# Round-by-round batched stage in the first memory layer, and an earlier fetch in the two linear layers

## The chip, the cores and the metric

The kernel runs on one NeuronCore of a Trainium2 chip. The metric is the device time of one execution in microseconds (us). The kernel before took 3794.12 us, the median of three runs (3792.07 to 3799.89). One further execution was profiled: its span is 3778.8 us, and its own time was 3780.49 us. All durations below are from that execution.

## The reference

Four layers are applied to x, 2048 rows of 640 numbers in bf16, each with a residual: A, B, A, B.

```
x = x + A(layernorm(x));  x = x + B(layernorm(x))
x = x + A(layernorm(x));  x = x + B(layernorm(x))

A: for each of 64 segments of 32 rows:
     h = concat(mem, xs)             # 8 memory rows + 32 rows
     q, k, v = h @ Wq, h @ Wk, h @ Wv    # 32 heads of 192
     p = softmax(mask(q k^T * scale)); o = (p v) @ Wo
     mem = o[:8]; out = o[8:]        # the next segment needs mem
B: linear attention over all 2048 rows, 32 heads of 20
```

A is a recurrence: the 8 memory rows of a segment come out of the segment before. But q, k and v of the rows of x do not depend on the memory, and no earlier row of a segment looks at its last 8 rows. So the kernel computes q, k and v of these 8 rows for all 64 segments at once, ahead of the recurrence, and keeps the 8 memory rows and the first 24 rows (32 in all) for the recurrence itself.

## The kernel before

Layer A has two stages.

The batched stage (`A_pre`) computes q, k and v of the last 8 rows of all 64 segments, in two halves `h` of 32 segments (256 rows each). The weights are cut into four rounds `r` of 8 heads. One half of one round is called a unit below: there are 8. A unit multiplies K and Q (L787, twelve PSUM banks, each copied out once by `evict`), stores them to DRAM with one DMA of 1536 KB issued on ScalarE (L793, `kqb`), then multiplies V (L804, eight banks) and stores it with eight DMAs on GpSimd (L808, `vb`). So a unit has 20 copies out of PSUM, which alternate between VectorE (L87) and ScalarE (L89), and PSUM gives the stage eight banks. Before: half 0 goes through rounds 0, 1, 2, 3, then half 1 through 3, 2, 1, 0. Weights come on SyncE's queue. Three of five blocks of each matrix of rounds 0 and 3 share storage ("slots", loaded at L611; the others at L617), so each change between these two rounds loads nine blocks of 384 KB again.

In the first layer the stage also does the layernorm. The rows of half 0 are gathered first (`gather`, L691: four DMAs of 32 rows for each 128 rows), normalised (L221 to L244: VectorE statistics, two GpSimd casts, ScalarE Ln and Exp, VectorE scale), turned by TensorE (L166) and copied (`pt`). The rows of half 1, and all 16 blocks of 128 rows for the second stage, are normalised by small tasks: each `evict` runs the next task of a list, four tasks to a block (load, statistics, Ln and Exp, scale and store). The list is filled when half 0 reaches its third round. So tasks run with the copies 41 to 112 of 160.

The second stage (`A_chain`) is the recurrence over 64 segments, some 21 us each; its work on TensorE takes most of the span. It starts when the batched stage has ended.

In a layer B the beginning finishes layer A: the attention output of the last 8 rows of each segment has still to be multiplied by Wo. That is done in four parts `tb` of 16 segments (`post_steps`): `fetch` loads 1536 KB (L1117) and spreads it with four copies (recorded at L87 and L89, the lines of `Ev.copy`), `multiply` does 96 matmuls (L1129, L1130), copies the result (L1132, L1133) and stores it to `attn` (L1135). The fetched block and its spread form have two places each, used in turn. Beside it the first 512 rows are loaded, added to `attn` on GpSimd (L360), normalised (`norm_rows`) and, after the third multiply, turned by TensorE (`turn_rows`, L166, four blocks `ps_x` in a pool of three PSUM banks, copied by ScalarE). The instruction order of layer B is made by a scheduler; in the two stages of A it is kept as written, apart from DMA placement.

Of the kernel before, what the change touches and what calls it, by code (L numbers as in the profile page):

```python
# [8 lines left out]
P = 128  # L9
BF16 = mybir.dt.bfloat16  # L10
F32 = mybir.dt.float32
# [104 lines left out]
class Kernel:  # L116
# [131 lines left out]
    def layer_B(self, x_dram, at_dram, xout_dram, xnext_dram, li, bp, post):  # L248


        nc, tc, KC, D = self.nc, self.tc, self.KC, self.Dm
# [41 lines left out]
        with tc.tile_pool(name=f"B{li}_kv", bufs=1, space=bass.MemoryType.PSUM, reuse_waits="tile") as kvp, \  # L293
# [71 lines left out]
            def turn_rows(b, xn, xnT):  # L365
                pt = bank("ps_x", BF16)
                for k in range(KC):
                    self.transp(out=pt[:, P * k:P * k + P], in_=xn[:, P * k:P * k + P], identity=self.ident[:, :])
                q = P * (b % 4)
                self.ev.copy(out=xnT[:, :, q:q + P], in_=pt[:, 0:D].rearrange("p (k t) -> p k t", t=P), eng="s")  # L370

# [83 lines left out]
            with tc.issue_after(self.last_load.ins):  # L455
                load_rows(0)
            fetch, multiply = post
            ow = [fetch(tb) for tb in range(2)]
            for j in (1, 2, 0):
                nc.sync.dma_start(out=wqkv[:, :, D * j:D * j + D],  # L460
                                  in_=self.B_wqkv.rearrange("(k p) n -> p k n", p=P)[:, :, D * j:D * j + D])
            multiply(0, ow[0], kv_ps[0], side_bank("ps_post"))
            ow.append(fetch(2))
            rows = [norm_rows(b) for b in range(4)]
            multiply(1, ow[1], kv_ps[1], side_bank("ps_post"))
            ow.append(fetch(3))
            multiply(2, ow[2], kv_ps[0], side_bank("ps_post"))
            first_xnT = new_xnT()
            for b in range(4):
                turn_rows(b, rows[b], first_xnT)  # L470
            multiply(3, ow[3], kv_ps[1], side_bank("ps_post"))
            waiting = None
            for g in range(NG):
                xnT = first_xnT if g == 0 else norm_T(g)
                if g == 1:
                    late_constants()
                keys_values(g, xnT)
                if waiting is not None:
                    query_features(*waiting)
                waiting = (g, heads_T(xnT, 0, "qT"))  # L480
# [179 lines left out]
    def A_pre(self, xn_dram, li, load_matrix, piece, wo_mid, wo_end, lay_out_wo, early_wo, x_raw):  # L660
# [12 lines left out]
        with ExitStack() as es:  # L673
# [13 lines left out]

            def gather(dst, src, h, k):
                xv = src.rearrange("(s t) d -> t s d", t=32)
                for t2 in range(TP):  # L690
                    (nc.gpsimd if k % 2 else nc.scalar).dma_start(out=dst[SH * t2:SH * t2 + SH, :], in_=xv[24 + TP * k + t2, SH * h:SH * h + SH])  # L691

            def columns(h):
                return xT[h][:, 0:KC * T].rearrange("p (b t) -> p b t", t=T)
# [57 lines left out]
            if x_raw is not None:  # L752
                first = [norm_tasks(lambda x, k=k: gather(x, x_raw, 0, k),
                                    lambda xn, k=k: normed.__setitem__((0, k), xn)) for k in range(NT)]
                for step in zip(*first):
                    for f in step:
                        f()
            turn = nv = 0
            for h in range(NH):
                xBT = columns(h)  # L760
                for k in range(NT):
                    if x_raw is not None:
                        xb = normed[h, k]
                    else:
                        xb = xB[h][k % 2]
                        gather(xb, xn_dram, h, k)
                    transpose_rows(xb, h, k)

                if h == NH - 1:
                    lay_out_wo()  # L770
                for ri, r in enumerate(range(NR) if h == 0 and NH > 1 else range(NR - 1, -1, -1)):
                    st = sts[turn % 2]
                    turn += 1
                    if x_raw is not None and h == 0 and ri == 1:
                        self.build_A_consts()
                    if x_raw is not None and h + 1 < NH and ri == 2:
                        tasks += tails(h + 1)
                        tasks += all_rows()
                    for mi, m in enumerate("KQ"):
                        load_matrix(m, r)  # L780
                        w = [piece(m, r, b) for b in range(KC)]
                        for c0 in range(0, 12, CB):
                            ps = ps_.tile([P, 512], F32, name="ps_pre", tag="bank")
                            for i in range(CB):
                                c = c0 + i
                                for b in range(KC):
                                    nc.tensor.matmul(ps[:, T * i:T * i + T], lhsT=w[b][:, P * c:P * c + P], rhs=xBT[:, b, :],  # L787
                                                     start=(b == 0), stop=(b == KC - 1))
                            G, xi = c0 // 6, c0 % 6
                            so = st[:, :, 96 * mi:96 * mi + 96].rearrange("p s (i g t) -> p i g s t", g=2, t=8)  # L790
                            evict(out=so[:, xi:xi + CB, G],
                                  in_=ps[:, :].rearrange("p (i t s) -> p i s t", i=CB, t=8))
                    nc.scalar.dma_start(out=self.kqb_d[SH * h:SH * h + SH, :, r, :].rearrange("s p f -> p s f"), in_=st)  # L793
                    load_matrix("V", r)
                    if h == NH - 1 and ri == NR - 1:
                        early_wo()
                    w = [piece("V", r, b) for b in range(KC)]
                    for k in range(NT):
                        vt = vts[nv % 2]
                        nv += 1  # L800
                        for g in range(4):
                            ps = ps_.tile([P, 512], F32, name="ps_pre", tag="bank")
                            for b in range(KC):
                                nc.tensor.matmul(ps[:, 0:384], lhsT=xBT[:, b, P * k:P * k + P],  # L804
                                                 rhs=w[b][:, 384 * g:384 * g + 384], start=(b == 0), stop=(b == KC - 1))
                            evict(out=self.two_heads(vt[:, g, :]), in_=ps[:, 0:384].rearrange("p (e f) -> p e f", e=2))
                        for t2 in range(TP):
                            nc.gpsimd.dma_start(out=self.vb_d[SH * h:SH * h + SH, r, :, TP * k + t2, :],  # L808
                                                in_=vt[SH * t2:SH * t2 + SH, :, :].rearrange("p (g x) f -> p g (x f)", x=2))
            assert not tasks  # L810
# [297 lines left out]
    def post_steps(self, ops):  # L1108
# [5 lines left out]
        def fetch(tb):  # L1114
            o = 7680 + 12288 * (tb % 2)
            ot = low[:, o:o + 6144].rearrange("p (s f) -> p s f", f=384)
            nc.sync.dma_start(out=ot, in_=self.otb_d[16 * tb:16 * tb + 16].rearrange("s p f -> p s f"))  # L1117
            ow = low[:, o + 6144:o + 12288].rearrange("p (c q) -> p c q", q=P)
            for k in range(4):
# [16 lines left out]

        return fetch, multiply

# [34 lines left out]
```

## Time and profile before

| what | value |
|---|---|
| runs, median | 3794.12 us (3792.07 to 3799.89) |
| profiled span | 3778.8 us |
| TensorE busy in the span | 3556.3 us (94%) |
| batched stage of the first layer | 0 to 213.75 us |
| its first unit starts on TensorE | 14.29 us |
| TensorE idle between 14.29 and 213.75 us | 28.7 us |
| beginning of the first layer B (four multiplies) | 1604.84 to 1668.53 us |
| beginning of the second layer B | 3466.51 to 3531.28 us |

A line of the profile's order of time reads: start, duration, engine, source line, operation, what it writes and reads, how often, and in brackets how long the engine had been idle before and what ended that. "SPq", "ACTq" and "POOLq" are DMA issues of those engines. A line of the table of stretches reads: stretch, length, then for PE (matmul), PEld (weight load), DVE, ACT and POOL the busy time and in brackets the number of instructions, then the granted TensorE clock, the DMA share and GB/s.

### The profile page before, as it was taken

What the parts mean: (1) busy time and instruction counts of PE and PEld (TensorE: products, weight loads), DVE (VectorE), ACT (ScalarE), POOL (GpSimd) and SP (SyncE); (2) the same over time, 40 slices, a digit from 0 to 9 for tenths busy, and PEclk for the clock granted to TensorE, in tenths of its full rate; (3) what the DMA queues carried; (4) which work ended last, traced back from release to release, by engine and by line L of the source; (5) the groups of instructions that cost most, each with busy time, mean ns of one, the idle gap of its engine ahead of it and who ended that gap; (6) DMA issues with size and microseconds to landing.
All of it is one profiled execution on the core that took longest, in us unless ns stands there. A gap on an engine that the chain in (4) does not pass through costs nothing. (4 is left out here: it accounts for less than half of the span.)

```text
span 3778.8 us, 169108 instructions
## 1 busy us (share of the span) xinstructions
PE 3556.3 (94%) x71080; PEld 2322.3 (61%) x71408; DVE 2363.3 (63%) x6290; ACT 2072.3 (55%) x5285; POOL 1664.9 (44%) x4367
## 2 busy tenths in 40 slices
PE   7889999999999999989899899999999999999898
PEld 5666666666666666645468566666666666665453
DVE  3546666666666666645643566666666666664565
ACT  2246666656666666536432566666666666664553
POOL 2435555555554555430242454555555554553300
PEclk9999999999999999989899999999999999999899
DMA  9788787878878888840377888888788888889100
GB/s 327 238 261 290 275 297 270 291 276 279 296 273 287 279 289 285 299 143 1 121 245 199 292 284 283 293 280 289 274 294 276 290 286 275 294 276 312 53 1 29
DMA packets 532613, 935.26 MB, mean 248 GB/s; under 512 B 141178, under 2 KB 298378, under 8 KB 531850
## 3 DMA queue, kind: packets, MB, share of 16 engines
q1 hardware_dynamic: 393898, 805.73, 60.6%
q0 software_dynamic: 68288, 88.95, 8.0%
q10 hardware_dynamic: 69664, 29.76, 3.0%
q8 instruction: 558, 9.14, 1.0%
q14 instruction: 205, 1.68, 0.1%
HBM read 855.97 MB, written 72.09 MB: 246 GB/s over the span
## 5 line engine op out<-in xcount | busy, mean ns | idle before, releaser
L885 PE MATMUL ps_qk<-arena,hT 128*32 128x384 bf16 x20480 | 1002.9, 328 | 21.3 <-DMA arena<-in_A_Wk_dram 7.2
L885 PEld LDWEIGHTS <-hT 128*32 128x32 bf16 x30720 | 739.0, 96 | 439.7 <-DVE hT L1103 28.6
L895 ACT ACTIVATE raw<-ps_qk 128x384 bf16<-128x384 f32 x1024 | 502.0, 490 | 393.3 <-PE ps_s L993 250.9
L961 PE MATMUL ps_w<-arena,OT 128*32 128x160 bf16 x24576 | 545.1, 234 | 30.0 <-issue 16.3
L868 POOL DMA_DIRECT2D Vp<-vb x512 | 258.7, 505 | 655.6 <-PE ps_o L935 447.9
L885 PE MATMUL ps_v<-arena,hT 128*32 128x384 bf16 x10240 | 535.3, 329 | 0.0
L961 PEld LDWEIGHTS <-OT 128*32 128x32 bf16 x24576 | 434.5, 97 | 127.1 <-issue 49.0
L900 DVE STREAM_TRANSPOSE KT<-raw 128x384 bf16<-128x384 bf16 x512 | 296.2, 578 | 201.3 <-ACT raw L895 197.3
L903 DVE STREAM_TRANSPOSE QT<-raw 128x256 bf16<-128x256 bf16 x512 | 227.9, 445 | 239.0 <-ACT raw L895 196.8
L856 POOL DMA_DIRECT2D kqb<-kqb x512 | 290.0, 567 | 165.7 <-POOL KT L864 147.5
L916 DVE CAST Vp<-ps_v 64x384 bf16<-64x384 f32 x512 | 286.3, 559 | 89.0 <-ACT Vp L914 76.2
L954 POOL DMA_DIRECT2D otb<-otb x512 | 282.4, 552 | 123.0 <-DVE otb L950 102.2
L914 ACT ACTIVATE Vp<-ps_v 64x384 bf16<-64x384 f32 x512 | 246.1, 481 | 146.6 <-PE ps_v L885 109.3
L941 DVE CAST OT<-ps_o 128x192 bf16<-128x192 f32 x512 | 183.0, 358 | 217.8 <-PE ps_o L935 200.2
L1000 DVE TENSOR_TENSOR E<-E,ps_s 80x320 bf16<-80x320 bf16 x512 | 247.6, 484 | 73.4 <-ACT ps_s L999 69.3
L979 ACT ACTIVATE E<-ps_s 80x320 bf16<-80x320 f32 x512 | 221.5, 433 | 127.1 <-PE ps_s L927 99.0
L935 PEld LDWEIGHTS <-Vp 80*128 80x128 bf16 x4096 | 183.1, 99 | 156.3 <-issue 122.2
L935 PE MATMUL ps_o<-E,Vp 80*128 80x80 bf16 x4096 | 233.7, 202 | 22.9 <-ACT Vp L914 4.1
L927 PE MATMUL ps_s<-QT,KT 128*80 128x80 bf16 (+1 forms) x3072 | 234.3, 214 | 20.2 <-DVE KT L900 11.3
L849 ACT ACTIVATE Vp<-ps_w 32x160 bf16<-32x160 f32 x512 | 150.3, 294 | 177.8 <-DVE wt L1102 160.6
L940 ACT ACTIVATE OT<-ps_o 128x192 bf16<-128x192 f32 x512 | 167.7, 328 | 141.2 <-PE ps_o L935 141.2
L927 PEld LDWEIGHTS <-KT 128*80 128x80 bf16 x3072 | 196.2, 119 | 68.6 <-issue 58.9
(148 smaller groups left out, 5474.4 us busy)
## 6 DMA issues: line engine op xcount, KB each, us to landing
arena<-wo_rows SPq DMA_DIRECT2D x792, 320.0 KB, 6.8
arena<-in_A_Wq_dram SPq DMA_DIRECT2D x430, 384.0 KB, 4.7
arena<-in_A_Wv_dram SPq DMA_DIRECT2D x430, 384.0 KB, 6.4
arena<-in_A_Wk_dram SPq DMA_DIRECT2D x768, 192.0 KB, 4.7
kqb<-arena ACTq DMA_DIRECT2D x16, 1536.0 KB, 8.7
kqb<-kqb POOLq DMA_DIRECT2D x512, 48.0 KB, 5.1
arena<-in_A_Wk_dram SPq DMA_DIRECT2D x46, 384.0 KB, 7.1
vb<-arena POOLq DMA_DIRECT2D x128, 112.0 KB, 5.5
```

The source lines that it names most:

```text
L856: nc.gpsimd.dma_start(out=kqb[:], in_=self.kqb_d[s, :, r, :])
L868: nc.gpsimd.dma_start(out=Vs[n % 2][64:80, :], in_=self.vb_d[s, r].rearrange("g t f -> (g t) f"))
L885: nc.tensor.matmul(o[32 * g:32 * g + 32, 0:384], lhsT=hT[:, b, :], rhs=rhs, start=(i == 0), stop=(i == KC - 1), tile_position=(0, 32 * g), ...
L895: nc.scalar.activation(out=raw[:], in_=ps[:, 0:384], func=ACT.Copy)
L900: nc.vector.transpose(out=KT[:, :, 0:64], in_=raw[:, :].rearrange("p (c j) -> p c j", j=64))
L914: nc.scalar.activation(out=o, in_=i, func=ACT.Copy)
L916: nc.vector.tensor_copy(out=o, in_=i)
L927: nc.tensor.matmul(S[0:80, c0:c0 + 80 * (q1 - q0)], lhsT=KT[:, 3 * x + i, :], rhs=QT[:, x, q0:q1, :], start=False, stop=(x == 1 and i == 2 ...
L935: nc.tensor.matmul(O[x][:, 80 * i:80 * i + 80], lhsT=Vs[n % 2][0:80, 448 * x + k:448 * x + k + 128], rhs=E[0:80, 160 * x + 80 * e:160 * x ...
L954: nc.gpsimd.dma_start(out=self.otb_d[s, :, 96 * r:96 * r + 96], in_=otb[:, :, :].rearrange("p c t -> p (c t)"))
L961: nc.tensor.matmul(W[32 * g:32 * g + 32, 0:160], lhsT=OT[:, c, q:q + 32], rhs=w[:, 640 * i + 160 * g:640 * i + 160 * g + 160], start=(firs ...
L1000: nc.vector.tensor_tensor(out=E[0:80, 0:320], in0=E[0:80, 0:320], in1=rc, op=ALU.mult)
```

## The change

1. In the first layer the order of units becomes round 3 half 0, round 3 half 1, round 2 half 0, round 2 half 1, and so on to round 0. Layer three (the second A) keeps its order.
2. The eight gathers of half 0 are issued alternately on SyncE's and ScalarE's queues, ahead of the weights in SyncE's queue. Before, four went on ScalarE's and four on GpSimd's.
3. The list of tasks is filled at the first unit, so tasks run with the copies 1 to 72. The masks (`build_A_consts`) are built at the third unit instead of the second, and the two DMAs that lay out part of Wo (`lay_out_wo`) are issued at the fifth unit of the new order.
4. In both layers B `fetch` is split into `fetch` (the DMA) and `spread` (the copies). All four fetches are issued ahead of the loads of `wqkv`. The normalisation of the second 512 rows (`norm_T(1)`) is put after the last copy of the first 512 turned rows.

```diff
-                    (nc.gpsimd if k % 2 else nc.scalar).dma_start(out=dst[SH * t2:SH * t2 + SH, :], in_=xv[24 + TP * k + t2, SH * h:SH * h + SH])
+                    e = queues[t2 % 2] if queues else nc.gpsimd if k % 2 else nc.scalar
+                    e.dma_start(out=dst[SH * t2:SH * t2 + SH, :], in_=xv[24 + TP * k + t2, SH * h:SH * h + SH])
...
-                first = [norm_tasks(lambda x, k=k: gather(x, x_raw, 0, k),
+                first = [norm_tasks(lambda x, k=k: gather(x, x_raw, 0, k, (nc.sync, nc.scalar)),
...
+            if x_raw is not None:
+                steps = [(h, ri, NR - 1 - ri) for ri in range(NR) for h in range(NH)]
+            else:
+                steps = [(h, ri, ri if h == 0 and NH > 1 else NR - 1 - ri) for h in range(NH) for ri in range(NR)]
...
-                if h == NH - 1:
-                    lay_out_wo()
+                if (h, ri) == ((NH - 1, 0) if x_raw is None else (0, 2)):
+                    lay_out_wo()
...
-                    if x_raw is not None and h + 1 < NH and ri == 2:
-                        tasks += tails(h + 1)
-                        tasks += all_rows()
+                if x_raw is not None and (h, ri) == (0, 0):
+                    for h1 in range(1, NH):
+                        tasks += tails(h1)
+                    tasks += all_rows()
...
-            fetch, multiply = post
-            ow = [fetch(tb) for tb in range(2)]
+            fetch, spread, multiply = post
+            ot = [fetch(tb) for tb in range(2)]
+            ow = [spread(tb, ot[tb]) for tb in range(2)]
+            ot += [fetch(tb) for tb in range(2, 4)]
...
-            ow.append(fetch(2))
+            ow.append(spread(2, ot[2]))
...
-                turn_rows(b, rows[b], first_xnT)
+                turned = turn_rows(b, rows[b], first_xnT)
...
-                xnT = first_xnT if g == 0 else norm_T(g)
+                if g == 0:
+                    xnT = first_xnT
+                elif g == 1:
+                    with tc.issue_after(turned.ins):
+                        xnT = norm_T(g)
+                else:
+                    xnT = norm_T(g)
```

The built instruction lists have the same number of rows on TensorE, and on the other engines they differ only in the batched stage of the first layer and in the beginnings of the two layers B. SyncE's list loses nine slot loads and gains four gathers; GpSimd's loses four gathers.

## The prediction

> **What bounds the kernel now.** I read the page's busy shares first: TensorE is busy 94% of the span, so only 3778.8 - 3556.3 = 222 us can be won without taking work from it, and the change takes none. Then I looked for where TensorE idles in the parts that the change touches: the table of stretches, the order of time around each gap, and the waits of the batched stage.
>
> The table of stretches, one line for each unit of the first layer's batched stage in the order before (half 0 with rounds 0 to 3, half 1 with 3 to 0):
>
> ```profile
> 14.29:36.04 21.75, 21.75 (x160) 16.76 (x160) 6.40 (x11) 5.05 (x9) 2.13 (x4) 1.00 1.03 400
> 36.04:55.64 19.60, 19.60 (x162) 15.66 (x160) 6.39 (x10) 5.43 (x10) 5.64 (x24) 1.00 0.90 293
> 55.64:88.26 32.62, 22.72 (x162) 16.96 (x160) 8.98 (x22) 4.51 (x11) 7.27 (x18) 0.84 0.94 328
> 88.26:122.02 33.76, 22.33 (x170) 17.25 (x170) 20.56 (x56) 10.91 (x31) 17.78 (x43) 0.84 0.74 203
> 122.02:144.51 22.49, 22.49 (x161) 17.00 (x161) 12.84 (x33) 5.96 (x14) 7.02 (x19) 0.87 1.02 356
> 144.51:169.22 24.71, 20.66 (x162) 15.61 (x161) 13.23 (x37) 6.60 (x19) 10.15 (x25) 1.00 0.74 240
> 169.22:193.99 24.77, 21.44 (x161) 16.36 (x160) 9.68 (x19) 6.32 (x13) 13.09 (x27) 0.93 0.65 169
> 193.99:213.75 19.76, 19.76 (x166) 15.62 (x167) 6.38 (x10) 5.54 (x10) 4.22 (x8) 1.00 0.70 196
> ```
>
> A unit without disturbance takes 19.6 to 19.8 us. Units three to seven, which carry the normalisation tasks or their end, take up to 33.8. In the order of time one sees why:
>
> ```profile
> 8.52 0.89 DVE L221 BATCH_NORM_STATS2 ln_stats<-ln_x 128x6 f32<-128x320 bf16 x2 [5.67 <-DMA ln_x<-in_A_x_dram]
> ...
> 66.01 7.84 ACTq L691 DMA_DIRECT2D ln_x<-in_A_x_dram  x4
> 73.90 1.08 ACT L89 ACTIVATE arena<-ps_pre 128x512 bf16<-128x512 f32 x2 [17.57 <-DMA ln_x<-in_A_x_dram]
> 74.55 4.43 PE L787 MATMUL ps_pre<-arena 128*128 128x256 bf16 x20 [7.82 <-ACT arena L89]
> ...
> 122.02 16.15 PE L787 MATMUL ps_pre<-arena 128*128 128x256 bf16 x120 [9.12 <-ACT arena L89]
> ```
>
> The first statistics wait for the gathered rows until 8.52 us. Later ScalarE stands 17.6 us at the four gathers of half 1, behind weight traffic; PSUM fills and TensorE waits 7.8 us. At 122 us it waits 9.1 us for the turned rows of half 1. Two lines of the waits in this stage:
>
> ```profile
> DVE ln_stats L221 <- DMA ln_x<-in_A_x_dram: 42.2, 10, 16.4
> SPq L617 <- DMA kqb<-arena: 26.9, 2, 14.0
> ```
>
> VectorE, which also empties PSUM, waited 42.2 us in ten times for rows; and SyncE's weight loads waited 26.9 us for stores of `kqb` with which they share no data. In the built lists, the DMAs of SyncE and ScalarE share eight completion semaphores in rotation, so each waits for the one eight before it.
>
> In each layer B the turned rows of block 3 need a PSUM bank, whose copy on ScalarE stands behind the Ln of the next 512 rows:
>
> ```profile
> 1649.53 0.29 ACT L234 ACTIVATE ln_lv<-ln_mvr,eps 128x1 f32<-128x1 f32 x1 [6.63 <-POOL ln_mvr L227]
> ...
> 1653.08 2.48 ACT L89 ACTIVATE arena<-ps_x 128x640 bf16<-128x640 bf16 x4
> ...
> 1653.83 0.69 PE L166 MATMUL ps_x<-ident,arena 128*128 128x128 bf16 x5 [8.65 <-ACT arena L89]
> ...
> 3515.68 0.69 PE L166 MATMUL ps_x<-ident,arena 128*128 128x128 bf16 x5 [8.84 <-ACT arena L89]
> ```
>
> **What the Trainium skill says.** "DMA: Bandwidth & Descriptors", Anatomy of one DMA, gives a DMA a fixed cost of about 2 us beside its bytes, most of it the receipt of the write. The trace agrees for an unloaded machine (the fastest row load landed after 2.5 us); under the weight stream the median is 5.7 and the slowest 10.8, and those decide here. "TensorE: Matmul & The Clock Gate", What's actually happening: an idle window of about 3.4 us halves the clock until as long a busy one. The trace agrees: after the 8.65 us gap the L1129 matmuls take 0.63 us instead of 0.38 for 2.7 us. So a removed gap is worth more than its length.
>
> **The change part by part.**
>
> *The two layers B.* Removed: gaps of 8.65 and 8.84 us, and the cold matmuls after them. The 95 matmuls that follow take 14.2 and 15.1 us; at the pace of the 288 before them (39.3 us, 0.1365 each) they would take 13.0; so 1.2 and 2.1. Together 20.8 us. Added: SyncE's list now has fetches 1, 2, 3, then `wqkv`, then the first store to `attn`. Fetch 3 must wait for the spread of block 1, which ended at 1613.07 + 2.86 = 1615.9; behind it wait the three `wqkv` loads (6.8 us of issue), and behind them the `attn` store (at 1618.8 before), four row loads (1.85 us) and the `attn` rows. `wqkv` is first read at 1668, so its delay costs nothing. The rows landed at 1628.65; I put them at 1636 (1615.9 + 6.8 + store and landing 3 + issues 3 + load 7). Block 3 is added last, some 6 us later (four adds at 1.4), and is ready 3.5 us after that: about 1646, against transposes due at 1644. With its copy and the next transposes this leaves a gap of about 3 us in each; bounds 0.5 (rows in time, one copy) and 4.5. Net gain 2 x (10.4 - 3) = 15 us, from 12 to 20. The later normalisation is not needed before its transposes at 1706.7, 38 us on: nothing.
>
> *The start.* The gathers no longer share DMA with weights: eight issues of 0.44 us on two queues end near 2.7 us; with 2.5 us to land, statistics start near 5.2 for block 1 (8.52 and 9.62 before). The steps from there to the first matmul took 14.29 - 9.62 = 4.7 us, so it starts near 10.2 us. The five K blocks (2 MB at 400 GB/s is 5 us after about 3) are there by 10. Gain 4 us, bounds 2 and 5. It counts only through the tasks, next.
>
> *The stage.* Evictions are the measure: 160, at 0.99 us each when nothing disturbs (19.8/20). Before, the last task ran at 168.6; TensorE had then done 120 of 160, and 40 x 0.99 + about 5 for the set-up waits of the seventh unit gives 213.2 (traced 213.75). The same for after: tasks end with copy 72, TensorE is at most eight banks ahead, so 80 x 0.99 + 5 = 84 us remain. When do the tasks end? The two gathered blocks of half 1 come first; ScalarE's gathers are now ahead of any `kqb` store, so the 17.6 us stand goes; their statistics start near 17. Before, the first of the 16 blocks followed 10.5 us after that (76.16 to 86.66) and the 16 took 82 us (86.66 to 168.6). At that pace they end at 17 + 10.5 + 82 = 109.5. But the first eight now run beside the weight stream. Blocks whose load took 6.5 us there were 6.9 to 7.4 us apart instead of the mean 5.1, though the next one then followed after 3.5 to 3.9; I add 2 us, and 3 us for the masks (eighteen small GpSimd operations, 39.1 to 42.1 us before), now in the middle of the tasks. The turn to half 1 and its 9 us are inside the 82 and stay, now after unit one. Tasks end near 114, the stage at 198: 15 us earlier. Bounds: with the best eight blocks' pace (4.5 us) 100 and 184, a gain of 30; at 6.5 us a block 131 and 215, a loss of 2. In the 6.5 stands one thing more: in the built list the second `kqb` store on ScalarE waits for a V block of the third weight round, the 44th of 60. By the bytes moved in the trace before (18.7 MB by 55 us, 25.7 by 74.5) that lands between 60 and 67 us, against 45 to 56 for the store; copies wait behind it.
>
> *No cost or gain.* The nine slot loads (3.5 MB, 9 us of DMA) lay ahead of their use; no TensorE wait names a weight. The layout of Wo on ScalarE still lands (20.8 us) before the eighth unit. The recurrence's first `kqb` load now waits for the seventh unit's store: 9.0 + 5.5 us, inside the eighth unit's 19.8. The second A is unchanged.
>
> Sum: 15 + 15 = 30 us, 3778.8 to 3748.8 for the traced execution, which lay 13.6 us below the median of its timed sisters. On the median: 3794.1 - 30 = 3764.
>
> **The rivals.** *All of it (B):* tasks at 4.5 us, B full: 30 + 19 = 49, 3745. For: four blocks in uncrowded stretches took 17.3 and 18.5 us. Against: the first half of the tasks now lies in the most crowded stretch. *Only the layers B (C):* the tasks beside the weight stream eat the stage's gain: 3794 - 15 = 3779. For: the 42.2 us of waits for rows. *Slower (D):* one mechanism, VectorE standing at its row statistics while weights stream. It outweighs the 15 us of the layers B and 7.6 more only if the tasks end past 213.75 - 84 + 22.6 = 152 us, or (152 - 28)/16 = 7.8 us for every block; the worst four in a row took 23.8 us, 6.0 each. Then about 3805. *Not what it says (E):* the gaps in the layers B stay because block 3 comes later still, and the stage breaks even: 3792.
>
> **How the numbers follow.** A measurement of this kernel can tell 0.2%, 7.6 us, from no change. Forecast (A) 0.52, B 0.2, C 0.16, D 0.06, E 0.06. Faster: A, B and nearly all of C, 0.87; same: E and the rest, 0.07; slower 0.06. The range runs from B's time, 3745, to 3784, which holds C and its neighbours: gains of 10 to 49, the sum of the parts' bounds being 10 to 50.
>
> **What would show it.** First matmul of the stage near 10 us; no ScalarE stand of 17 us at gathers; the last row statistics near 111 us; the stage's end near 198; at ps_x gaps of 1 to 4 us in place of 8.7; the first spread of fetched block 2 after its landing near 1620. Wrong if the last statistics come past 130, if ps_x still waits 8 us, or if the recurrence, 21.7 us a segment, changes its pace.

## The result, and the profile after

The changed kernel takes 3771.39 us (median of four runs, 3766.23 to 3776.69) against 3793.1 us for the kernel before on the same chip: a ratio of 0.9942, with a 95% interval from 0.9918 to 0.9966. Timed once more beside later experiments it gave 0.9944 (0.9922 to 0.9966). So it is faster by 21 to 22 us, and the interval reaches from 13 to 31. The forecast was 30 us, a time of 3764.

The profiled execution spans 3764.5 us, 14.3 less than that of before. Where the stretches of the two traces differ:

| stretch, us | before | after | difference |
|---|---|---|---|
| start of the first unit on TensorE (inside the next line) | 14.29 | 10.19 | -4.1 |
| end of the batched stage, first layer | 213.75 | 198.01 | -15.7 |
| recurrence 1 | 1391.1 | 1396.3 | +5.2 |
| four multiplies, first layer B | 63.7 | 56.2 | -7.5 |
| rest of that layer B | 255.0 | 259.1 | +4.1 |
| batched stage of the second A | 160.0 | 160.0 | 0 |
| recurrence 2 | 1382.9 | 1386.6 | +3.7 |
| four multiplies, second layer B | 64.8 | 60.75 | -4.0 |
| rest of that layer B | 247.5 | 247.5 | 0 |

Not all of this is the change. Over fourteen traces of this study the two recurrences together took from 2767 to 2791 us, with no relation to which parts were in: stage_only below has 2780, a second trace of the changed kernel 2782, another variant 2767. Their 5.2 and 3.7 us are spread. The 15.7 us are not, as the experiments show. The rest of the first layer B lies anywhere from 255.6 to 264.3 us in seven traces with the changed layers B, so its 4.1 us alone would say little; but they hold a new gap, shown below.

The table of stretches of the changed kernel, its first six units (round 3 half 0, round 3 half 1, round 2 half 0, and so on):

```profile
10.19:40.48 30.29, 22.65 (x171) 17.42 (x171) 14.77 (x38) 8.18 (x21) 8.64 (x24) 0.92 1.05 380
40.48:62.62 22.14, 22.14 (x161) 16.81 (x161) 12.73 (x33) 5.08 (x12) 6.92 (x18) 0.88 0.95 338
62.62:91.87 29.25, 22.07 (x161) 16.46 (x160) 12.57 (x34) 6.50 (x18) 12.76 (x42) 0.94 0.98 358
91.87:115.53 23.66, 21.14 (x160) 15.56 (x160) 15.91 (x44) 7.97 (x23) 11.29 (x28) 1.00 0.72 206
115.53:139.12 23.59, 20.08 (x161) 15.62 (x160) 9.68 (x19) 6.15 (x13) 9.05 (x17) 1.00 1.04 315
139.12:158.72 19.60, 19.60 (x162) 15.64 (x160) 6.38 (x10) 5.54 (x10) 4.21 (x8) 1.00 0.68 201
```

The tasks now lie in the first four units, and from the sixth on a unit takes 19.6 us. The worst units were 32.6 and 33.8 us before and are 30.3 and 29.3 now. The clock column matters too: over the first 250 us its mean went from 0.911 to 0.945, and 0.034 x 250 / 3778.8 = 0.0022 is most of the rise of the mean clock between the kernels (from 0.9769 in 21 executions of the kernel before to 0.9795 in six of the changed one in the same session). It goes with the stage: in the two traces with the old stage it is 0.911 over these 250 us, in the twelve with the new one 0.925 to 0.952.

In the order of time, the same places as in the prediction:

```profile
3.48 0.89 DVE L221 BATCH_NORM_STATS2 ln_stats<-ln_x 128x6 f32<-128x320 bf16 x2 [0.64 <-DMA ln_x<-in_A_x_dram]
...
16.86 0.89 DVE L221 BATCH_NORM_STATS2 ln_stats<-ln_x 128x6 f32<-128x320 bf16 x2 [0.17 <-DMA ln_x<-in_A_x_dram]
...
40.48 15.80 PE L803 MATMUL ps_pre<-arena 128*128 128x256 bf16 x120 [7.64 <-ACT arena L89]
...
68.76 0.87 ACT L89 ACTIVATE arena<-ps_pre 128x384 bf16<-128x384 f32 x2 [9.42 <-DMA arena<-in_A_Wv_dram]
...
111.91 0.88 DVE L221 BATCH_NORM_STATS2 ln_stats<-ln_x 128x6 f32<-128x320 bf16 x2
```

Statistics start at 3.5 instead of 8.5 us, those of half 1 at 16.9, the last come at 111.9 instead of 165.6. The 17.6 us stand at the gathers is gone. In its place ScalarE stands 9.4 us before 68.76, and what ends it is a landed block of Wv: the second `kqb` store waits for a weight load with which it shares no data, as forecast. VectorE's waits for rows fell from 42.2 us to this, in the waits of the stage:

```profile
DVE ln_stats L221 <- DMA ln_x<-in_A_x_dram: 17.9, 12, 3.1
```

In the two layers B, at the turned rows of the third and the fourth block of 128 rows (blocks 2 and 3):

```profile
1635.43 0.45 PE L166 MATMUL ps_x<-ident,arena 128*128 128x128 bf16 x5 [1.52 <-ACT arena L246]
1637.37 0.44 PE L166 MATMUL ps_x<-ident,arena 128*128 128x128 bf16 x5 [1.26 <-ACT arena L89]
...
3499.10 0.45 PE L166 MATMUL ps_x<-ident,arena 128*128 128x128 bf16 x5 [3.27 <-ACT arena L246]
3501.04 0.69 PE L166 MATMUL ps_x<-ident,arena 128*128 128x128 bf16 x5 [1.26 <-ACT arena L89]
```

The gaps of 8.65 and 8.84 us became 1.52 + 1.26 = 2.8 and 3.27 + 1.26 = 4.5. But a new gap stands 30 us further on. Here are GpSimd, VectorE and TensorE of the first layer B:

```profile
1657.58 4.02 POOL L328 TENSOR_SCALAR_AFFINE_SELECT arena<-arena 128x720 bf16<-128x720 bf16 x4
1661.57 5.43 POOL L360 TENSOR_TENSOR arena<-arena 128x640 bf16<-128x640 bf16 x4
1662.99 0.89 DVE L221 BATCH_NORM_STATS2 ln_stats<-arena 128x6 f32<-128x320 bf16 x2 [5.06 <-POOL arena L360]
1664.76 1.47 DVE L409 TENSOR_REDUCE sk<-arena 128x64 f32<-128x1280 bf16 x1
1668.01 0.47 PE L428 MATMUL kv<-arena 128*120 128x126 bf16 x2 [5.27 <-DVE arena L422]
```

The first `kv` matmul waits 5.27 us for VectorE. VectorE's next product for it, the sums at L409, is queued behind statistics (L221) which wait for GpSimd's additions (L360) of the last 512 rows, and those are queued behind constants that GpSimd builds for layer B (L317 to L328, 8.3 us in all). Here are GpSimd's first constant and TensorE's first `kv` matmul in the kernel before, and the same constant after:

```profile
1667.07 1.38 POOL L317 MEMSET arena<- 128x1536 bf16 x1 [0.78 <-PE kv L1129]
1681.87 0.46 PE L428 MATMUL kv<-arena 128*120 128x126 bf16 x2 [1.06 <-DVE arena L422]
...
1653.22 1.38 POOL L317 MEMSET arena<- 128x1536 bf16 x1
```

Before, the matmul waited 1.06 us, and GpSimd itself waited for TensorE's multiplies: L317 starts 1.5 us before they end. After, it follows GpSimd's own casts without a gap, 2.8 us after the multiplies have ended. The multiplies end 7.5 us earlier than before, counted from their start, L317 starts only 3.3 us earlier. The difference of 4.2 us is the new gap and the +4.1 in the table.

### The profile page after: what moved, and what is told of

Same layout as the page of the kernel before. It is cut to its first block, busy times and chain, and to the rows that moved or that the text cites. A ratio compares the mean times of both kernels' runs of the same rounds, so it can differ in the third digit from the quotient of the medians.

```text
span 3764.5 us, 169123 instructions
## 1 busy us (share of the span) xinstructions
PE 3547.2 (94%) x71064; PEld 2322.7 (62%) x71408; DVE 2365.1 (63%) x6290; ACT 2072.6 (55%) x5285; POOL 1658.2 (44%) x4363
## 4 chain that ended last, share of the span: by engine, by line
PE 56%; DMA 12%; DVE 8%; issue 8%; ACT 6%; PEld 4%; POOL 4%; SPq 0%; POOLq 0%; DVEq 0%; ACTq 0%
PE ps_qk L901 18%; PE ps_w L977 8%; PE ps_v L901 7%; DMA arena<-wo_rows 5%; PE ps_o L951 4%; PE ps_s L943 4%; PEld L803 3%; DVE hT L857 3%; PE ps_s L1009 2%; DMA Vp<-vb 2%; PE ps_s L938 2%; PE ps_idle L984 2%; PE ps_qk L388 2%; PE ps_pre L803 1%; DVE E L1016 1%
## 5 line engine op out<-in xcount | busy, mean ns | idle before, releaser
L932 DVE CAST Vp<-ps_v 64x384 bf16<-64x384 f32 x512 | 286.1, 559 | 90.0 <-ACT Vp L930 76.3
L1016 DVE TENSOR_TENSOR E<-E,ps_s 80x320 bf16<-80x320 bf16 x512 | 247.5, 483 | 73.3 <-ACT ps_s L1015 69.3
L943 PEld LDWEIGHTS <-KT 128*80 128x80 bf16 x3072 | 196.1, 120 | 71.3 <-issue 59.4
```

Of the source, the lines that this page charges most:

```text
L932: nc.vector.tensor_copy(out=o, in_=i)
L943: nc.tensor.matmul(S[0:80, c0:c0 + 80 * (q1 - q0)], lhsT=KT[:, 3 * x + i, :], rhs=QT[:, x, q0:q1, :], start=False, stop=(x == 1 and i == 2 ...
L1016: nc.vector.tensor_tensor(out=E[0:80, 0:320], in0=E[0:80, 0:320], in1=rc, op=ALU.mult)
```

## The experiments

Each run is given as a ratio to the kernel before on its own chip, since one of the chips was faster for both. Differences in us are worked out from the ratios.

| run | ratio, 95% interval | us | stage end | idle B1 | idle B3 |
|---|---|---|---|---|---|
| changed kernel, first | 0.9942 (0.9918 to 0.9966) | -22 | 198.0 | 42.2 | 29.3 |
| stage_only | 0.9973 (0.9960 to 0.9985) | -10 | 200.9 | 43.5 | 33.0 |
| layersB_only | 0.9992 (0.9984 to 1.0001) | -3 | 212.9 | 40.3 | 28.6 |
| issue_only | 0.9974 (0.9960 to 0.9988) | -10 | 199.2 | 42.5 | 33.3 |
| fetch_only | 0.9966 (0.9955 to 0.9978) | -13 | 198.6 | 41.1 | 32.3 |
| old_gathers | 0.9968 (0.9958 to 0.9979) | -12 | 201.9 | 41.0 | 28.9 |
| late_store | 0.9956 (0.9942 to 0.9970) | -17 | 196.1 | 40.7 | 27.7 |
| masks_late | 0.9958 (0.9943 to 0.9972) | -16 | 198.6 | 41.1 | 31.0 |
| consts_early | 1.0018 (1.0010 to 1.0027) | +7 | 198.8 | 54.4 | 36.0 |
| after_again | 0.9944 (0.9922 to 0.9966) | -21 | 198.3 | 41.7 | 30.3 |
| consts_dve | 0.9927 (0.9906 to 0.9947) | -28 | 198.9 | 39.4 | 28.5 |
| combo_w | 0.9934 (0.9911 to 0.9958) | -25 | 196.1 | 40.0 | 28.6 |
| rows_late | 0.9957 (0.9945 to 0.9970) | -16 | 197.9 | 41.7 | 29.6 |

"Idle" is the sum of TensorE's gaps between matmul records from the first multiply of the layer B to the first matmul of the next batched stage, or to the end of the run (43.5 and 32.4 us before); it leaves out the clock, which moves the length of a layer B by several us from one execution to the next. The times of single executions of one kernel lie up to 26 us apart, so a traced stretch decides below where a few us are asked for.

**stage_only.** The changed stage with the old layers B.

```diff
-            ot = [fetch(tb) for tb in range(2)]
-            ow = [spread(tb, ot[tb]) for tb in range(2)]
-            ot += [fetch(tb) for tb in range(2, 4)]
+            ow = [spread(tb, fetch(tb)) for tb in range(2)]
...
-                elif g == 1:
-                    with tc.issue_after(turned.ins):
-                        xnT = norm_T(g)
```

> Only the changes in the first layer's batched stage (order of units, gathers, task list); both layers B as before. My theory, that the two parts are independent and add up: the stage ends at 198 us as in the changed kernel, the gaps of 8.7 us at ps_x in both layers B are back, and the time falls by 15 us (11 to 19) against the kernel before. Rival, that a busier TensorE in the stage is paid back in the recurrence (4 us more between the first segment and the first layer B in the changed kernel's trace): the recurrence is again 4 us longer than before and the gain is 11 us or less. Rival, that those 4 us are only spread between executions: the recurrence lies anywhere from -4 to +5 us of before's, with no relation to which parts are in.

Measured: 10 us faster (6 to 15), the stage ends at 200.9 (198.0 to 199.2 in six other traces with the same stage), the gaps at `ps_x` are back with 9.27 and 9.46 us. The recurrences took 1390.6 and 1389.4 us: nothing of a payback in the first. Its rest of the first layer B took 259.3 us with the same idle time as before (43.5); here it is the pace of the matmuls, not a wait, that differs.

**layersB_only.** The old stage with the changed layers B.

The edit is the layer B part of the change, as its diff shows it, on the kernel before.

> Only the changes in the two layers B; the batched stage as before. My theory: stage ends at 213.8 us, the four multiplies take 56 us in the first and 61 us in the second layer B (63.7 and 64.8 before), the time falls by 11.5 us as the traces of before and after show (15 as predicted). Rival of the payback: the first recurrence is as before (nothing in the stage changed) and the 4 us in the rest of the first layer B (the stretch after the multiplies, 255.0 before and 259.1 after) come with the later normalisation of rows 512 to 1023, so only 7 us are gained. Rival of the spread: the rest of the layer B is within 1 us of 255.

Measured: 3 us faster at best guess, between 6 faster and 0.4 slower. The multiplies took 59.5 and 57.6 us, so the gaps fell as in the changed kernel. But the new gap in front of `kv` is there, 3.06 and 3.44 us, and the rest of the first layer B took 258.1. The rival that the gain is partly given back behind the multiplies is right in its result; its reason, the later normalisation, is taken up further on. Together with stage_only this makes 13 us, 8 less than the changed kernel measured twice; their intervals overlap, and no run tells whether the two parts help each other or the executions drew apart.

**issue_only and fetch_only.** Half of the change of the layers B each: only the later normalisation (issue_only: the three lines of `fetch` and `spread` as in the diff of stage_only), or only the early fetches (fetch_only):

```diff
-                elif g == 1:
-                    with tc.issue_after(turned.ins):
-                        xnT = norm_T(g)
```

> The changed kernel, with fetches 2 and 3 back at their old places and only the normalisation of the second 512 rows put later. My theory: ScalarE's copy of the turned block no longer stands behind the Ln, which was the whole gap of 8.7 us; the rows of attn land earlier (1629 instead of 1636 on before's scale), so block 3 is there in time and the gap at ps_x is only 1.3 us, with none in front of the L246 result; but fetch 2 then starts behind wqkv as before, hidden. The time is 2 to 5 us below the changed kernel's, the multiplies take 55 to 57 us in both layers B. Rival, that the early fetches are what removes the gap: the gap is 5 us or more and the time is 5 to 8 us above the changed kernel's in each layer B.

> The changed kernel, with the fetches early but the normalisation of the second 512 rows not put later. My theory: the copy of ps_x stands behind the Ln again, the gap is 8 us or more in each layer B, and as the early fetches win nothing by themselves (they were hidden) and delay the rows of attn, the time is 12 to 20 us above the changed kernel's. Rival, that the early fetches carry the gain: the gap stays below 3 us and the time is that of the changed kernel, within 4 us.

Both missed their numbers. The first lines are TensorE of fetch_only:

```profile
1632.96 0.45 PE L166 MATMUL ps_x<-ident,arena 128*128 128x128 bf16 x5 [1.69 <-ACT arena L246]
1639.08 0.69 PE L166 MATMUL ps_x<-ident,arena 128*128 128x128 bf16 x5 [5.45 <-ACT arena L89]
```

The next are ScalarE and TensorE of issue_only:

```profile
1649.35 0.29 ACT L234 ACTIVATE ln_lv<-ln_mvr,eps 128x1 f32<-128x1 f32 x1 [6.25 <-POOL ln_mvr L227]
1651.97 1.56 ACT L89 ACTIVATE arena<-ps_qk 120x512 bf16<-120x512 f32 x3
1652.61 2.72 PE L388 MATMUL ps_qk<-arena 128*120 128x512 bf16 x6 [6.28 <-ACT arena L89]
```

Without the later normalisation 7.1 us of the 8.7 remain. With it alone the gap at `ps_x` is gone altogether, the multiplies take 53.5 us in both layers, and 6.3 us come back at `ps_qk`: ScalarE's copies of those banks now stand behind the Ln of the third 512 rows, which wait for their rows of `attn`. Idle time is then that of the kernel before (42.5 and 33.3 against 43.5 and 32.4). It is the same blocking, one group of rows later. Only both halves together leave less idle time in both layers. A count from a common start says the same: from the first multiply to the first `kv` it is 77.7 and 78.0 us in issue_only, 76.3 and 76.6 in fetch_only, 77.0 to 78.8 in two traces with the old layers B, and 73.3 to 75.2 in seven with both halves.

**old_gathers.** The gathers of half 0 where they were.

```diff
-                first = [norm_tasks(lambda x, k=k: gather(x, x_raw, 0, k, (nc.sync, nc.scalar)),
+                first = [norm_tasks(lambda x, k=k: gather(x, x_raw, 0, k),
```

> The changed kernel, with the eight gathers of half 0 back on ScalarE's and GpSimd's queues. My theory: the first matmul of the stage starts near 14 us instead of 10.2, the tasks start 4 us later and the last row statistics come near 116 us instead of 112, so the stage ends at 202 us instead of 198 and the time is 4 us above the changed kernel's. Rival, that the start is hidden: the tasks are bound by the loads of rows and the weight stream from 20 us on, the last row statistics stay at 112 us and the stage ends within 1 us of 198.

TensorE of its beginning:

```profile
14.35 15.29 PE L803 MATMUL ps_pre<-arena 128*128 128x256 bf16 x120 [0.79 <-ACT arena L89]
```

The stage ends at 201.9. The start moved by 2.9 to 4.2 us and the end by 3.6 to 3.9 against the changed kernel's two traces (starts at 10.19 and 11.44, ends at 198.0 and 198.3). Five more traces with the new gathers and the same stage end at 198.6 to 200.9, so the end alone would not decide. Counted from its first matmul the stage takes 187.6 us here and 186.9 to 189.7 in those seven traces: it is no shorter for the late start. The start is not hidden. The last row statistics came at 113.8 us and not near 116, so about half of the delay was made up there, and the end moved all the same.

**late_store.** The second unit's `kqb` store, issued behind the third unit's K copies.

```diff
-                nc.scalar.dma_start(out=self.kqb_d[SH * h:SH * h + SH, :, r, :].rearrange("s p f -> p s f"), in_=st)
+                    while held and mi == 0:
+                        held.pop()()
+                def store(h=h, r=r, st=st):
+                    nc.scalar.dma_start(out=self.kqb_d[SH * h:SH * h + SH, :, r, :].rearrange("s p f -> p s f"), in_=st)
+                if x_raw is not None and (h, ri) == (1, 0):
+                    held.append(store)
+                else:
+                    store()
```

> The changed kernel, with one DMA moved in ScalarE's list: the store of kqb of the second unit is issued behind the third unit's K copies, instead of ahead of the second unit's V copies, where ScalarE stood 9.4 us until 67.9 us. My theory, that the stand and the copies queued behind it delay the tasks: the stand is gone or below 2 us, the last row statistics come 7 us (4 to 9) earlier, at 105 us, and the stage ends 7 us (4 to 9) earlier, at 191. Rival, that the stand only takes the place of waits for the rows under the weight stream: the wait of VectorE for ln_x, 17.9 us in the changed kernel, grows by as much, and the stage ends within 2 us of 198. Rival, that the store meets its lane again: the stand comes back later, with the same end.

The stand of 9.4 us is gone, and the stage ends at 196.1: 2 us earlier than in the changed kernel's first trace and 3 earlier than the mean of the seven traces with its stage (199.0), not 7. The rival is mostly right. The waits of the stage show where the rest went:

```profile
DVE ln_stats L221 <- DMA ln_x<-in_A_x_dram: 22.1, 13, 4.4
ACT arena L89 <- DVE ln_stats L221: 3.3, 1, 3.3
ACT arena L89 <- DMA arena<-in_A_Wq_dram: 2.6, 1, 2.6
```

VectorE's wait for rows grew by 4.2 us, and two short stands of ScalarE at `kqb` stores, 3.3 and 2.6 us, came in (the view puts them down to other instructions, but each ends with the issue of a `kqb` store, at 88.33 and 80.32 us). A stand of 9.4 us was worth 2 to 3.

**masks_late.** The masks built behind the tasks.

```diff
-                if x_raw is not None and h == 0 and ri == 1:
+                if x_raw is not None and h == 0 and ri == 2:
                     self.build_A_consts()
```

> The changed kernel, with the masks (build_A_consts, 3.3 us of GpSimd at 77 us, between the casts of the tasks) built at the fifth unit, behind the tasks. My theory, with the 3 us of the prediction: the last row statistics come 3 us earlier, at 109, and the stage ends at 195. Rival, that GpSimd has slack there (it waits 2 us or more for VectorE's statistics in most blocks): the last row statistics stay within 1 us of 112 and the stage's end within 1 us of 198.

The last statistics came 0.9 us earlier (111.0), the stage ended at 198.6 against 198.0 and 198.3; both lie within the spread of the traces. The rival is right: GpSimd has slack there, and the 3 us of the prediction are nothing.

**rows_late.** The tasks of the 16 blocks listed later.

```diff
                     for h1 in range(1, NH):
                         tasks += tails(h1)
+                if x_raw is not None and (h, ri) == (0, 1):
                     tasks += all_rows()
```

> The changed kernel, with the tasks for the 16 blocks listed at the second unit (the eight tasks of half 1 stay in the first), so that they lie with copies 21 to 84 instead of 9 to 72 and fewer of them beside the weight stream. Theory A, that each block has its price wherever it lies: the last row statistics come 12 copies later, at 121 to 124 us, with 68 copies x 0.99 + 5 us left the stage ends at 195 to 198, within 3 us of the changed kernel's. Theory B, that the weight stream makes the tasks dearer (the 2 us of the prediction and the stand at the store): the stage ends 4 us or more earlier, at 194 or less. Theory C, that TensorE idles in the first unit for want of tasks, no matter where they are: it ends later, at 201 or more.

The text misnames the place: (0, 1) is the third unit, so these tasks lie with the copies 41 to 104, and its 121 to 124 us don't apply. The last statistics came at 147.0. Still the stage ends at 197.9, within 0.4 us of the changed kernel, which is theory A's result. Its reason, one price for a block wherever it lies, is not shown: two gaps changed places. Here are TensorE and VectorE:

```profile
33.71 13.26 PE L804 MATMUL ps_pre<-arena 128*128 128x256 bf16 x120 [0.79 <-ACT arena L89]
...
72.33 0.89 DVE L221 BATCH_NORM_STATS2 ln_stats<-ln_x 128x6 f32<-128x320 bf16 x2 [14.86 <-DMA ln_x<-in_A_x_dram]
74.07 9.01 PE L821 MATMUL ps_pre<-arena 128*128 128x384 bf16 x40 [7.50 <-DVE arena L87]
```

At the turn to half 1 TensorE waits 0.79 us. In the changed kernel it waits 7.64 us there (until 40.48), since VectorE's copy of turned rows stands behind the statistics of a block, which wait for their rows. In exchange TensorE waits 7.50 us until 74.07, when VectorE has stood 14.86 us for the first of the 16 blocks. That the two gaps are equal is chance. On balance the place of these 64 tasks is worth nothing here, so filling the list earlier with them is not what shortened the stage; the eight tasks of half 1 stayed in the first unit, where the new order needs them.

**consts_early and consts_dve.** Two ways to take the constants from in front of GpSimd's last additions. The first builds them right behind the casts of block 3, in other storage (`osum` and `expd` moved to where the first fetched block lay); the second puts memsets and copies on VectorE.

```diff
+            with tc.issue_after(self.last_cast.ins):
+                late_constants()
             multiply(3, ow[3], kv_ps[1], side_bank("ps_post"))
```

```diff
-                nc.gpsimd.memset(osum[:], 0.0)
+                nc.vector.memset(osum[:], 0.0)
...
-                        nc.gpsimd.tensor_copy(out=o, in_=bcast_mid(blk[:, 0:nh], 2))
+                        nc.vector.tensor_copy(out=o, in_=bcast_mid(blk[:, 0:nh], 2))
...
-                nc.gpsimd.memset(expd[:], 0.0)
+                nc.vector.memset(expd[:], 0.0)
```

> The changed kernel, with the constants of layer B (8.3 us of memsets, copies and selects on GpSimd, ahead of the additions of rows 1024 to 1535) built right behind the casts of block 3, in storage that is free by then; the table of what lies where in layer B is changed for that. My theory, that the 4.1 us more in the rest of the first layer B after are GpSimd, which is 4.2 us later relative to TensorE since the second normalisation was moved: the gap of 5.27 us in front of the first kv matmul falls to 1.1 and the rest of the first layer B to 255 us, 4 us less than in the changed kernel; the second layer B gains less than 1 us. Rival, that the gap is VectorE's own order: it stays above 4 us. Rival, that the constants now delay the additions of block 4 to 7 and so the turned rows of the second group: a new gap of 2 us or more in front of its ps_x or ps_qk.

> The changed kernel, with the memsets and copies of the constants of layer B (4.3 us of GpSimd's 8.3) put on VectorE; the selects stay. My theory, that the gap in front of the first kv matmul (3.1 to 5.3 us in the first layer B of six traces with the new order, 1.1 before) is VectorE's statistics waiting for GpSimd's additions of rows 1024 to 1535, which stand behind the constants: the gap falls by the 4.3 us, to 1.1 us in the first layer B, and from 1.8 to 3.4 to 1.1 in the second; 3 to 6 us in all, within the spread of the timed runs. Rival, that VectorE's own order sets it: the gap stays at 3 us or more, or grows by the 2 us that VectorE gets more.

(By their count the additions named there are those of rows 1536 to 2047.) consts_early was a loss, 7 us slower than the kernel before. There is no gap at `kv` above 1.1 us any more, but new ones of 3.8 us at `ps_qk` and 4.8 at `ps_pk` in the first layer B, 3.6 and 3.5 in the second, as its second rival has it, and TensorE waits 12.35 us instead of 4.3 for the last rows at the start of the second A; the cause of that one was not followed. consts_dve has the better time. Its GpSimd and TensorE:

```profile
1657.10 4.03 POOL L328 TENSOR_SCALAR_AFFINE_SELECT arena<-arena 128x720 bf16<-128x720 bf16 x4 [3.58 <-DVE arena L325]
1661.10 5.44 POOL L360 TENSOR_TENSOR arena<-arena 128x640 bf16<-128x640 bf16 x4
1667.13 0.27 PE L428 MATMUL kv<-arena 128*120 128x126 bf16 x2 [0.82 <-POOL arena L414]
```

The gap is 0.82 us instead of 5.01, but `kv` came no earlier: it starts 74.4 and 74.2 us after the first multiply in the two layers, and 73.3 to 75.2 in the seven traces with the constants on GpSimd. The multiplies ended later in this execution (61.3 us instead of 56.5, with a `ps_x` gap of 3.49 instead of 1.60), which leaves less to wait for. GpSimd also stood 3.58 us for VectorE's part, so most of the 4.3 us was not saved: from GpSimd's additions of the third 512 rows to the first `kv` it is 21.2 us in both layers, against 22.3 to 23.0 in the seven traces. So the constants are shown to be worth 1 to 2 us of the wait, not all of it. Idle time fell by 2.3 and 1.9 us against after_again. It is the fastest kernel measured, 28 us below the one before (20 to 36), but its interval overlaps that of the changed kernel.

**combo_w.** consts_dve, late_store, and the loads of `wqkv` behind the first additions:

```diff
             rows = [norm_rows(b) for b in range(4)]
+            for j in (1, 2, 0):
+                nc.sync.dma_start(out=wqkv[:, :, D * j:D * j + D],
+                                  in_=self.B_wqkv.rearrange("(k p) n -> p k n", p=P)[:, :, D * j:D * j + D])
             multiply(1, ow[1], kv_ps[1], side_bank("ps_post"))
```

> Three edits on the changed kernel together: constants' memsets and copies on VectorE as in the run before, the second unit's store of kqb late, and in layer B the three loads of wqkv traced behind the additions of the first 512 rows, so that the first store to attn no longer stands behind them on SyncE. Theory: the rows of attn land 4 to 7 us earlier, the gap at ps_x in front of block 3 (1.5 and 3.3 us in the changed kernel) is gone and only the 1.3 us for a bank is left; the kv gap is 1.1; the stage ends at 196. 8 to 12 us below the changed kernel in the traces' TensorE idle, and the fastest of all. Rival: the loads of wqkv come too late for the first ps_qk, with a gap of 3 us or more there, and nothing is won in the layers B.

25 us below the kernel before, not the fastest. The gap at `ps_x` is gone and the stage ends at 196.1, but at `ps_qk`:

```profile
1646.09 5.84 PE L388 MATMUL ps_qk<-arena 128*120 128x512 bf16 x15 [4.00 <-ACT arena L89]
```

The rows came early enough (additions 22.8 us after the first multiply instead of 28.4), and the wait moved again to ScalarE's copies behind the Ln of the third 512 rows, as in issue_only; it is not `wqkv` that it waits for, against the rival's reason, though the rival's result came true.

**after_again.** The changed kernel once more.

> The changed kernel once more, unaltered, timed beside the next three. If the parts add up as the first experiments measured them (the stage alone 10 us, interval 6 to 15; the layers B alone 3 us, interval 0 to 6), it lies 13 us below the kernel before (8 to 18), not 22. If the four executions of the first measurement were typical, 20 to 24 us below. In its trace the gap of 5 us in front of the first kv matmul of the first layer B is there again, and the stage ends at 198 us.

21 us below the kernel before, as the first time; the `kv` gap of its first layer B is 5.01 us, the stage ends at 198.3.

## Why the prediction was right and where it was not

*The direction and the size.* 30 us were forecast and 21 to 22 measured; the range held. The stage was right by its trace, the layers B were about half of what was said.

*The start.* Forecast 10.2 us, traced 10.19; the other traces with the new gathers have 10.6 to 11.4, so the last digit is luck. old_gathers shows that the earlier start reaches the end of the stage.

*The stage.* Forecast: half-1 statistics near 17 (16.9), last statistics near 111 (111.9), end at 198 (198.0, the earliest of seven traces with this stage; the latest is 200.9). By the trace the stage gives its 15 us; the timed stage_only gives 10, with 15 at the edge of its interval. Two terms of the sum were wrong and about cancelled, which is luck. The 3 us for the masks are none. The `kqb` store's wait came as described, until 67.85 us (60 to 67 forecast), but stood only in the bound; it costs 2 to 3 us. And the logic that the end follows from where the tasks end was wrong: with the 64 tasks later the last statistics came 35 us later and the end stayed, and in old_gathers they came 2 us later and the end 4.

Of the 15.7 us the start explains 4.1. The other 11.6 are, in the two traces, 7.9 us less of gaps (28.7 before, 20.8 after) and 3.7 us less for the same 1290 matmul records, at a mean clock of 0.96 instead of 0.92. The gap of 7.8 us that TensorE had at the gathers of half 1 has no counterpart after. This points to the new order of units, which brings these gathers ahead of every store. It is read from the traces and by elimination: no run had the new order alone. Forecast D, VectorE standing at its statistics, was far off: the longest stand was 3.1 us.

*The layers B: the step that failed.* The sum said: 8.65 + 8.84 us of gaps and 3.3 us of cold clock removed, gaps of about 3 us each left, 15 net. At the end of the multiplies most of this is there: the gaps left are 2.8 and 4.5, and the multiplies are 7.5 and 4.0 us shorter; the gain by the clock shows only in the first. Block 3 is ready at 1647.1 on the clock of the trace before (its L246 ends at 1636.56, and 10.56 us lie between the starts of the multiplies), forecast was 1646. Two terms cancelled in this: the additions began at 1633 instead of 1636, and from them to block 3 it took 13.9 us instead of about 10.

What failed is that the sum ends there and puts all that follows at nothing. It asked when TensorE needs the later rows ("38 us on: nothing"), and not what else TensorE meets on the way. The first `kv` matmul hangs on GpSimd: in all 22 layers B of the eleven traces in which GpSimd builds the constants behind its casts, it starts 14.8 us after L317, with the old layers B as with the new. As long as the gap at `ps_x` is long (the kernel before, stage_only, fetch_only), L317 waits for the multiplies, and so a shorter gap there is gained in full. With shorter multiplies GpSimd's own chain of rows, additions, casts and constants decides, and that came only 3.3 us earlier. The later normalisation did not hold GpSimd up: its additions of the second 512 rows began 36.6 us after the first multiply, 40.2 before and 37.0 in fetch_only, which lacks that line.

The price is a gap at `kv` of 3.1 to 5.3 us in the first layer B and 1.8 to 3.4 in the second, over seven traces with the changed layers B, against 1.1 before. Counted from the first multiply, the first `kv` comes 3.9 us earlier in the mean of these traces than in the two with the old layers B, some 8 us for both layers. Idle time fell from 43.5 to 41.2 and from 32.7 to 29.3 us in the same means, 5.7 us; with the clock, the two layers B are 4.7 + 5.0 = 9.7 us shorter. The timed layersB_only says 0 to 6. So the term of 15 should have been 3 to 10.

*What cost nothing.* The slot loads, the layout of Wo and the first `kqb` load of the recurrence were put at nothing, and the last three units of the stage run at 19.6 to 19.7 us each. The second A's stage is 160.0 us in both. The recurrences differ by no more than they do between executions.

## What to carry to other kernels

When a gap of one engine is closed, ask what that engine meets next, and how much earlier the other engine's chain gets there. Here the multiplies ended 7.5 us earlier, GpSimd's constants started only 3.3 us earlier, and the rest came back as a new gap one group of rows later. A distance between two instructions of different engines that stays the same over many traces (14.8 us from L317 to the first `kv`) is a sign that one chain binds them. When an edit makes a gap vanish, count from a common start whether the work behind it came earlier; in consts_dve it did not. A long stand of an engine is worth only what the next limit leaves of it, 2 to 3 of 9.4 us here, so price it by taking it away. Where executions of one kernel spread by half a per cent, judge a step by its own stretch of several traces and the sum by many timed runs.

## What the hardware showed that was not expected

- The row loads beside the weights took longer than those at the start. In the changed kernel the four gathers on SyncE's queue in the first 3 us landed after 1.9 us in the median (40 KB each), the 16 block loads on GpSimd's queue after 5.8 us (160 KB each). "DMA: Bandwidth & Descriptors", Anatomy of one DMA, in the Trainium skill puts the fixed cost of a DMA issued by GpSimd near 2 us; the fastest block load before, 2.5 us, is near that, and it ran from 105.0 to 107.6 us, where the DMA share was 0.37. Most block loads here are far above it. The 14.86 us in rows_late are no slow load: GpSimd issued it at 66.91 us, behind eight stores of `vb` and the masks, and it landed 5.4 us later.
- The mean granted clock differs between executions of one kernel and goes with their time: in the 44 executions of the kernel before in one session the correlation is -0.4 and the slope -16 us for 0.01 of clock.
- The stand of the `kqb` store at a weight load confirms in the trace that DMAs of ScalarE can wait for loads of SyncE with which they share no data (9.4 us, ended by a block of Wv).
